# Second chunk's probabilities in fp32 through TensorE, a second engine for the weights' high half, later notices of the other branch

## Chip, cores and metric

One core of one Trainium2 chip. The metric is the device time of one execution in microseconds (us). Engines are named as in the profile: PE is TensorE, DVE VectorE, ACT ScalarE, POOL GpSimd, SP SyncE, whose queue issues the DMAs.

## The reference

Causal sliding-window attention with sink keys (4 sequences, 8 heads, 768 positions, 64 channels a head, window 128, 4 sinks), followed by a two-layer feed-forward part (512 to 2048 to 512, ELU) on all 3072 tokens, in fp32.

```python
scores = scale * np.matmul(q, k.transpose(0, 1, 3, 2))
...
keep = is_sink | in_window
scores = np.where(keep, scores, -1000000000.0)
a = np.exp(scores - np.max(scores, axis=-1, keepdims=True))
a = a / (np.sum(a, axis=-1, keepdims=True) + 1e-09)
attn_out = np.matmul(a, v)
...
h = x @ w_in
g = np.where(h > 0.0, h, alpha * (np.exp(np.minimum(h, 0.0)) - 1.0))
out = g @ w_out
```

## The kernel before

The 3072 tokens are 24 tiles of 128, in nine chunks (`SIZES`): three of two tiles, then six of three. For each chunk `attention(c)` fills the `x` tiles (one for each of the 4 head pairs), and `feed_forward(c, f0, f1, start)` runs the feed-forward part over 16 slices `f` of 128 hidden channels. Chunk 0 and chunk 1 interleave their slices (`PARTS`): slices 0 to 6 of chunk 0, 0 to 12 of chunk 1, then the rest of both.

*Precision.* Products that matter are kept exact to nearly fp32 by splitting each operand into an fp16 high half and an fp16 rest, and adding three of the four partial products. The 32 weight pieces (`weights(k)`, two for each slice) come as fp64 words: ACT makes fp16 upper bits (L307), DVE joins them with the lower bits into an fp32 tile `wv` (L308), ACT copies that into the fp16 high half (L456), and POOL subtracts twice 256 columns for the low half (L457). A load waits until piece k - 5 is done (`AHEAD`).

*Attention of a tile-pair* (a query tile for two heads). A query tile sees its own key tile and the one before (`nb` = 1 in a sequence's first tile, else 2), each with 4 sink columns ahead of it (`KW` = 132); from the third tile of a sequence on (`t >= 2`) the sinks count separately. TensorE makes scores (L601, fp32, in chunks 0 to 3; L595 and L596, fp16, after), DVE adds the mask and takes the minimum (L616), ACT takes the exponential with its sum (L618), ACT or POOL scales the sum (L622), DVE takes the reciprocal (L623). Then there are two ways:

- Chunks with `c < PLAIN` (chunk 0 alone, whose tiles have t = 0 and 1) stay in fp32. POOL multiplies the identity by the reciprocals (`diagonal`, L630), TensorE multiplies the exponentials by that diagonal, which transposes and scales them into an accumulator bank `acc` (L636; banks 0 and 1 in turn, ring `tp`), ACT or DVE brings them to SBUF (L640), and TensorE multiplies them by the loaded fp32 values `vs` (L653).
- All others split. ACT writes the fp16 high half of the scaled probabilities (L668), DVE the rest (L669), POOL the sinks' halves (L675 multiplies, L678 casts, L679 subtracts), all side by side in `pq`; one DMA transpose (L687, issued by SP) turns them into `pt`; TensorE multiplies with the fp16 halves `vh` and `vl` of the values (L701, 12 products for two key blocks) and the sinks (L706, 2 products). `vh` and `vl` are made once for each key tile by ACT (L549) and DVE (L550) from `vs`, which SP loads into a ring of two buffers (L538); `sink_rows` does the same for the sinks of a sequence (L561 to L563).

A head pair's sum in bank `po` becomes the fp16 halves of `x` (ACT L739, DVE L740). In the feed-forward part TensorE makes `h` (L765, 12 products), ACT the exponential (L773), POOL or DVE a step (L775), DVE another (L776), ACT the fp16 high half of `g` (L779), POOL the rest (L786), and TensorE adds to the accumulators `acc` (L793). At a chunk's end the accumulators are stored (L816 to L819).

*What sets the order.* Nothing is ordered by hand. `Plan` collects tasks with an engine, an assumed duration, dependencies and rings of buffers; `order()` lists them through a model of the engines, eight rounds, each with due times worked out backwards from TensorE's order, and keeps the best. On TensorE tasks have positions (`pos`) and four lines (feed-forward, scores, values, transposing), each in its own order. A task may have a second engine (`or_`), and the model takes the one that is free. `slow` over 1 marks DVE tasks that the model delays while POOL works. The assumed durations (`act_us`, `dve_us`, `pool_us`, `PE_T`, `PE_V` and numbers at each task) thus decide the order of every queue. `with_idle_products` puts products of a constant tile (L882) into gaps that the plan shows in the first 100 us.

*The end.* A flag made from range checks decides between this result and a general path. Each engine loads it (L1141) and branches (L1142). `keep_order` gives each engine a notice of the branch's target (`BRANCH_PREFETCH_HINT` in the trace) a number of tasks before its last (`HINTS`).

## Time and profile before

| | us |
|---|---|
| device time, median of 3 runs | 631.98 (630.8 to 632.0) |
| profiled execution's own time | 632.12 |
| its span, first to last instruction | 630.3 |
| PE, DVE, ACT, POOL busy | 608.5, 451.4, 418.8, 291.2 |

The profile is of one execution. Busy time is that of an engine's instructions; idle time is put down to what released it. Matmuls overlap, so that records of one group can be longer than the distance between their starts. The chain of waits gives the time that each piece holds up the end. PEclk is the granted share of TensorE's clock. In instruction rows, "x" gives the number of records.

### The profile page before, as it was taken

The numbers are of one execution on the slowest core, as the hardware profiler recorded it, in microseconds if no ns is written. First come the engines' busy times: TensorE is split into PE (matmuls) and PEld (weight loads), VectorE is DVE, ScalarE is ACT, GpSimd is POOL, SyncE is SP. The second block draws the span as 40 slices with busy tenths as digits, with TensorE's granted clock in tenths as the row PEclk, the third lists the DMA queues.
The fourth block names the chain that finished last, engine by engine and source line by source line (L and its number), as shares of the span: only waits on it lengthen the run. The fifth ranks groups of instructions, "written<-read, shape, count | busy, mean of one in ns | idle before, by whom it ended". The sixth has DMA issues, their size and how long they took to land.

```text
span 630.3 us, 13327 instructions
## 1 busy us (share of the span) xinstructions
PE 608.5 (97%) x4504; PEld 357.1 (57%) x4504; DVE 451.4 (72%) x1187; ACT 418.8 (66%) x1192; POOL 291.2 (46%) x586
## 2 busy tenths in 40 slices
PE   6897999999999999999999999999999999999995
PEld 4564665666666555555555555555555555555552
DVE  7876677868678766688788889788778887542223
ACT  5888887978678866677667767676776676332221
POOL 4885699864345444344334444334334444222221
PEclk9998999999999999999999999999999999999998
DMA  8697967656546765486458865676556854511001
GB/s 288 212 254 189 305 233 208 161 165 176 120 120 137 194 104 103 88 220 174 103 168 189 208 158 148 145 193 144 154 118 134 220 130 100 124 56 30 0 2 54
DMA packets 120863, 95.06 MB, mean 151 GB/s; under 512 B 98132, under 2 KB 98132, under 8 KB 120788
## 3 DMA queue, kind: packets, MB, share of 16 engines
q1 hardware_dynamic: 120788, 94.14, 58.5%
q8 instruction: 37, 0.61, 0.4%
q14 instruction: 38, 0.31, 0.2%
HBM read 63.18 MB, written 7.34 MB: 112 GB/s over the span
## 4 chain that ended last, share of the span: by engine, by line
PE 90%; POOL 4%; DVE 2%; issue 2%; DMA 1%; ACT 0%; POOLq 0%; DVEq 0%; ACTq 0%
PE acc L793 39%; PE h L765 38%; PE po L701 5%; PE s L601 3%; PE s L595 2%; PE s L596 2%; POOL w L457 2%; DMA pt<-pq 1%; PE h L882 1%; DMA vs<-in_vx_dram 1%; POOL pq L630 1%; PE po L706 1%; DVE pt L334 0%; PE acc L636 0%; DVE wv L308 0%
## 5 line engine op out<-in xcount | busy, mean ns | idle before, releaser
L765 PE MATMUL h<-x,w 128*128 128x384 f16 (+1 forms) x1728 | 275.0, 309 | 1.5 <-DVE g L776 1.5
L765 PEld LDWEIGHTS <-w 128*128 128x128 f16 x1728 | 167.8, 98 | 94.9 <-issue 3.4
L786 POOL TENSOR_TENSOR gl<-g,gh 128x384 f16<-128x384 f32 (+1 forms) x144 | 126.0, 876 | 164.1 <-ACT gh L779 142.4
L793 PE MATMUL acc<-w,gh 128*128 128x512 f16 x768 | 192.8, 379 | 1.0 <-POOL w L457 1.0
L773 ACT ACTIVATE g<-h 128x384 f32<-128x384 f32 (+1 forms) x144 | 65.2, 453 | 102.2 <-PE h L765 93.0
L793 PEld LDWEIGHTS <-gh 128*128 128x128 f16 x768 | 72.4, 98 | 70.8 <-ACT g L773 1.4
L793 PE MATMUL acc<-w,gl 128*128 128x512 f16 x384 | 109.2, 379 | 0.0
L669 DVE SCALAR_TENSOR_TENSOR pq<-e,st,pq 128x256 f16<-128x256 f32 (+1 forms) x176 | 95.5, 569 | 15.0 <-ACT pq L668 14.7
L618 ACT ACTIVATE e<-e,st 128x264 f32<-128x264 f32 (+1 forms) x192 | 92.9, 485 | 14.9 <-DVE st L616 14.0
L779 ACT ACTIVATE gh<-g 128x384 f16<-128x384 f32 (+1 forms) x144 | 69.5, 482 | 45.2 <-DVE g L776 43.3
L616 DVE CUSTOM_DVE_ANT_0 e<-s,m 128x264 f32<-128x264 f32 (+1 forms) x192 | 71.8, 405 | 32.8 <-PE s L596 21.5
L776 DVE SCALAR_TENSOR_TENSOR g<-g,h 128x384 f32<-128x384 f32 (+1 forms) x144 | 72.9, 506 | 14.2 <-POOL g L775 12.4
L668 ACT ACTIVATE pq<-e,st 128x256 f16<-128x256 f32 (+1 forms) x176 | 77.5, 482 | 5.1 <-DVE st L623 4.3
L775 POOL TENSOR_SCALAR g<-g 128x384 f32<-128x384 f32 (+1 forms) x79 | 43.2, 547 | 79.1 <-ACT g L773 75.8
L775 DVE TENSOR_SCALAR g<-g 128x384 f32<-128x384 f32 (+1 forms) x65 | 27.1, 417 | 69.0 <-ACT g L773 68.9
L793 PEld LDWEIGHTS <-gl 128*128 128x128 f16 x384 | 37.5, 98 | 46.7 <-POOL gl L786 0.9
L457 POOL TENSOR_TENSOR w<-wv,w 128x256 f16<-128x256 f32 x64 | 48.9, 786 | 6.1 <-ACT w L456 5.5
L524 ACT ACTIVATE kq<-kqs 128x912 f16<-128x912 f32 (+1 forms) x40 | 35.8, 912 | 15.9 <-PE s L596 13.6
L622 POOL TENSOR_SCALAR st<-st 128x2 f32<-128x2 f32 x76 | 19.1, 251 | 49.4 <-ACT e L618 46.0
L701 PE MATMUL po<-pt,vh 128*64 128x128 f16 x656 | 36.1, 222 | 3.4 <-DVE x L740 1.9
L618 ACT ACTIVATION_READ_ACCUMULATOR e<-e,st 128x1 f32 x192 | 36.1, 188 | 0.0
L701 PEld LDWEIGHTS <-vh 128*64 128x64 f16 x656 | 26.6, 109 | 14.6 <-issue 14.0
(92 smaller groups left out, 619.4 us busy)
## 6 DMA issues: line engine op xcount, KB each, us to landing
raw<-in_wt_dram SPq DMA_DIRECT2D x32, 512.0 KB, 4.6
...
```

The source lines that it names most:

```text
L616: red = add("DVE", 0.24 + 0.001 * wd, lambda ee=ee, me=me, sp=sps[e], m=m, wd=wd, to_score=to_score: nc.vector.tensor_tensor_reduce(ee, sp ...
L618: ex = add("ACT", 0.47 + 0.00085 * wd, lambda ee=ee, me=me, rs=rs[:, e : e + 1]: nc.scalar.activation(ee, ee, AF.Exp, bias=me, scale=-1.0, ...
L668: a = add("ACT", act_us(nb * P, True), lambda src=src, hi=hi, re=re: nc.scalar.activation(hi, src, AF.Copy, scale=re), deps=[rr])
L669: b = add("DVE", 0.478 if nb == 2 else 0.33, lambda src=src, hi=hi, lo=lo, re=re: nc.vector.scalar_tensor_tensor(lo, src, re, hi, ALU.mult ...
L701: nc.tensor.matmul(po[e * D : (e + 1) * D, oc], vts[i][x][:, vo : vo + D], pt[:, (2 * e + part) * nb + i, :], start=new, stop=last)
L765: nc.tensor.matmul(hp[:, :n], win[:, part, d, :], xx[:, :n], start=k == 0, stop=k == 3 * ND - 1)
L773: a = add("ACT", act_us(n) + 0.18, lambda gf=gf, hp=hp, sums=sums: nc.scalar.activation(gf, hp[:, :n], AF.Exp, scale=1.0 / G_SCALE, accum_ ...
L775: b = add("DVE", 0.14 + 0.00057 * n, lambda gf=gf: nc.vector.tensor_scalar(gf, gf, -1.0, G_SCALE, ALU.add, ALU.mult), deps=[a], slow=2.1, ...
L776: b = add("DVE", dve_us(n), lambda gf=gf, hp=hp: nc.vector.scalar_tensor_tensor(gf, gf, 0.0, hp[:, :n], ALU.min, ALU.max), deps=[b])
L779: th = add("ACT", act_us(n), lambda gf=gf, gh=gh: nc.scalar.activation(gh[:, :n], gf, AF.Copy), deps=[b])
L786: tls.append(add("POOL", pool_us(cut), lambda gl=gl, gf=gf, gh=gh, cut=cut: nc.gpsimd.tensor_tensor(gl[:, :cut], gf[:, :cut], gh[:, :cut], ...
L793: nc.tensor.matmul(acc[i], gg[:, i * P : (i + 1) * P], wout[:, part, :], start=f == f0 and k == 0, stop=f == f1 - 1 and k == 2)
```

## The change

- `PLAIN` goes from 1 to 2: chunk 1 (tiles with t = 2 and 3) keeps its probabilities in fp32 like chunk 0. Its transposed probabilities go to accumulator bank 2, one buffer (`tp1`).
- Since these tiles have separate sinks, there are new tasks: POOL scales the sinks' exponentials, TensorE transposes them into the free half of bank `po`, ACT or DVE brings them out, and a fifth value product (`sk_raw` by `sink_p`) adds them. The fp32 sink rows (8 partitions) are loaded once for the sequence (`sink_raw`).
- `vs` has four buffers instead of two.
- The copy into the weights' high half may run on ACT or DVE.
- Assumed durations change: `PE_T`, `PE_V`, the weight tasks, the diagonal, the sinks, the making of `x`.
- `HINTS`: 40 tasks instead of 120 before the end on ACT and DVE, 8 instead of 25 on SP.

```diff
 VISIT = 3
 DUP = 4
 AHEAD = 5
-PLAIN = 1
+PLAIN = 2
 IDLE_US, IDLE_FILL, IDLE_UNTIL, IDLE_LEAST = 0.11, 0.6, 100.0, 0.8
 V_AT = 7
 V_AT0 = 5.0
 T_AT = 3.5
-PE_T, PE_V = 0.25, 0.25
-RINGS = dict(tp=2, tp_=2, kqs=2, kq=3, vs=2, vm=2, vt=6, sk=2, e=3, st=6, pq=3, pt=6, g=2, gh=3, x=7, wv=4, s=2, po=1, h=2, wu=2, sv=2, wps=1, raw=6)
+PE_T, PE_V = 0.17, 0.11
+RINGS = dict(tp=2, tp_=2, kqs=2, kq=3, vs=4, sp=2, tp1=1, turned0=1, turned1=1, vm=2, vt=6, sk=2, e=3, st=6, pq=3, pt=6, g=2, gh=3, x=7, wv=4, s=2, po=1, h=2, wu=2, sv=2, wps=1, raw=6)
 
 
 def key_tiles(ch):
...
     vh = rows("vh", [P, VT], F16, RINGS["vt"])
     vl = rows("vl", [P, VT], F16, RINGS["vt"])
     sks = rows("sk", [P, VT], F16)
+    sps_ = rows("sp", [2 * NS, P], F32)
     vm = rows("vm", [P, NP, TOK_MAX], F32)
     es = rows("e", [P, 2, 2 * KW], F32)
     sts = rows("st", [P, 4 + 2 * NS], F32)
...
         ld = add("SP", 0.4, lambda: load_weights(nc, raw, wt[k]), deps=[w_done.get(k - AHEAD, [None])[0]], lat=1.45)
         if wide:
             steps = weight_f32(nc, v, top, raw, 2.0)
-            a = add("ACT", act_us(512), steps[0], deps=[ld])
-            b = add("DVE", 0.13 + 0.00108 * 512, steps[1], deps=[a], slow=1.5)
+            a = add("ACT", 0.77, steps[0], deps=[ld])
+            b = add("DVE", 0.8, steps[1], deps=[a], slow=1.5)
             ring("wu", [a], [b])
             ring("raw", [ld], [a, b])
         else:
             a = b = add("ACT", act_us(512), lambda: nc.scalar.activation(v, raw[:, :512].bitcast(F32), AF.Copy, scale=W_SCALE), deps=[ld])
             ring("raw", [ld], [a])
 
-        th = add("ACT", act_us(512), lambda: nc.scalar.activation(w[k][:, 0, :], v, AF.Copy), deps=[b])
-        tls = [add("POOL", pool_us(256), lambda c=c: nc.gpsimd.tensor_tensor(w[k][:, 1, c], v[:, c], w[k][:, 0, c], ALU.subtract), deps=[th]) for c in (slice(0, 256), slice(256, 512))]
+        th = add("ACT", act_us(512), lambda: nc.scalar.activation(w[k][:, 0, :], v, AF.Copy), deps=[b], slow=2.0, or_=("DVE", 0.13+0.0006*512, lambda: nc.vector.tensor_copy(w[k][:, 0, :], v)))
+        tls = [add("POOL", 0.75, lambda c=c: nc.gpsimd.tensor_tensor(w[k][:, 1, c], v[:, c], w[k][:, 0, c], ALU.subtract), deps=[th]) for c in (slice(0, 256), slice(256, 512))]
         tl = tls[-1]
         ring("wv", [b], tls)
         w_done[k] = th, *tls
...
         x_old.append((lo, hi, users))
 
     later = []
-    raw_of, v_of, sk_of = {}, {}, {}
+    raw_of, v_of, sk_of, raw_sinks = {}, {}, {}, {}
 
     def attention(c):
         ts = CHUNKS[c]
...
                 sk_of[b] = sk, vb, users
             return sk_of[b]
 
+        def sink_raw(b):
+
+            if b not in raw_sinks:
+                st = pool.tile([2 * NS, VT], F32, name=f"sinks{b}")
+                o = SINKS + b * VT
+                raw_sinks[b] = st, add("SP", 0.4, lambda: nc.sync.dma_start(st, vx[0 : 2 * NS, o : o + VT]), lat=0.1)
+            return raw_sinks[b]
+
         k = 0
         for p in range(NP):
             kqp = [split_keys(2 * p + e) for e in range(2 if c >= DUP else 1)]
...
                 rr = add("DVE", 0.17, lambda rs=rs: nc.vector.reciprocal(rs, rs), deps=[rr])
                 if c < PLAIN:
                     dg = pq[:, :4, :].rearrange("p b k -> p (b k)").bitcast(F32).rearrange("p (e k) -> p e k", e=2)
-                    tp = acc[slot("tp")]
+                    tp, tp_ring = (acc[slot("tp")], "tp") if c == 0 else (acc[2], "tp1")
                     ptf = pt.rearrange("p b k -> p (b k)").bitcast(F32)[:, : 2 * nb * P]
+                    far = t >= 2
+                    turned_sinks, sink_p = po[0 : 2 * NS, (nt + j) * P : (nt + j + 1) * P], sps_[slot("sp")][0 : 2 * NS, :] if far else None
 
                     def diagonal(dg=dg, rs=rs):
                         nc.gpsimd.tensor_tensor(dg, ident.unsqueeze(1).to_broadcast([P, 2, P]), rs.unsqueeze(2).to_broadcast([P, 2, P]), ALU.mult)
...
                                 o = (e * nb + i) * P
                                 nc.tensor.matmul(tp[:, o : o + P], e3[:, e, i * KW + NS : (i + 1) * KW], dg[:, e, :], start=True, stop=True)
 
-                    dgs = add("POOL", pool_us(2 * P), diagonal, deps=[rr])
+                    dgs = add("POOL", 0.8, diagonal, deps=[rr])
                     tr = add("PE", PE_T * 2 * nb, turned, deps=[dgs], pos=at[k] + T_AT, line=3)
                     ev = add("ACT", act_us(2 * nb * P), lambda ptf=ptf, tp=tp, n=2 * nb * P: nc.scalar.activation(ptf, tp[:, :n], AF.Copy), deps=[tr, rest_ if pt is pts[-1] else None], or_=("DVE", dve_us(2 * nb * P), lambda ptf=ptf, tp=tp, n=2 * nb * P: nc.vector.tensor_scalar(ptf, tp[:, :n], 1.0, None, ALU.mult)))
-                    ring("e", [r for r, _ in exps], [tr])
-                    ring("st", [r for r, _ in exps], [dgs])
+                    readers, evs = [dgs], [ev]
+                    if far:
+                        sk_raw, sk_ld = sink_raw(g // NT)
+                        sn = add("POOL", 0.25, lambda tmp=tmp, e3=e3, rs=rs: nc.gpsimd.tensor_tensor(tmp, e3[:, :, 0:NS], rs.unsqueeze(2).to_broadcast([P, 2, NS]), ALU.mult), deps=[rr], lock=False)
+                        ts_ = add("PE", 0.2, lambda o=turned_sinks, tmp=tmp: nc.tensor.matmul(o, tmp.rearrange("p e k -> p (e k)"), ident, start=True, stop=True), deps=[sn], pos=at[k] + T_AT + 0.01, line=3)
+                        se = add("ACT", 0.28, lambda o=turned_sinks, sink_p=sink_p: nc.scalar.activation(sink_p, o, AF.Copy), deps=[ts_], or_=("DVE", 0.27, lambda o=turned_sinks, sink_p=sink_p: nc.vector.tensor_scalar(sink_p, o, 1.0, None, ALU.mult)))
+                        readers += [sn, ts_]
+                        evs += [se, sk_ld]
+                        ring("turned" + str(j), [ts_], [se])
+                    ring("e", [r for r, _ in exps], [tr] + readers[1:2])
+                    ring("st", [r for r, _ in exps], readers)
                     ring("pq", [dgs], [tr])
-                    ring("tp", [tr], [ev])
-                    evacs[slot("tp_")] = ev
+                    ring(tp_ring, [tr], [ev])
+                    evacs[slot("tp_") if c == 0 else 2] = ev
                     vts = [vraw(g - nb + 1 + i) for i in range(nb)]
 
-                    def values(po=po, vts=vts, ptf=ptf, j=j, nb=nb, p=p):
+                    def values(po=po, vts=vts, ptf=ptf, j=j, nb=nb, p=p, far=far, sink_p=sink_p, sk_raw=sk_raw if far else None):
                         oc = slice(j * P, (j + 1) * P)
                         for i in range(nb):
                             for e in range(2):
                                 vo = p * P + e * D
-                                nc.tensor.matmul(po[e * D : (e + 1) * D, oc], vts[i][0][:, vo : vo + D], ptf[:, (e * nb + i) * P : (e * nb + i + 1) * P], start=j == 0 and i == 0, stop=j == nt - 1 and i == nb - 1)
-
-                    val = add("PE", PE_V * 2 * nb, values, deps=[ev, *(v[1] for v in vts)], pos=at[k - j + nt - 1] + V_AT0 + 0.01 * j, line=2)
+                                nc.tensor.matmul(po[e * D : (e + 1) * D, oc], vts[i][0][:, vo : vo + D], ptf[:, (e * nb + i) * P : (e * nb + i + 1) * P], start=i == 0, stop=i == nb - 1 and not far)
+                        if far:
+                            nc.tensor.matmul(po[:, oc], sk_raw[:, p * P : (p + 1) * P], sink_p, start=False, stop=True)
+
+                    val = add("PE", PE_V * 2 * nb + (0.2 if far else 0.0), values, deps=[*evs, *(v[1] for v in vts)], pos=at[k - j + nt - 1] + V_AT0 + 0.01 * j, line=2)
                     ring("pt", [ev], [val])
+                    if far:
+                        ring("sp", [se], [val])
                     vals.append(val)
                     for v in vts:
                         v[2].append(val)
...
 
             xh, xl = x_room(qc)
             to_x = X_SCALE / P_SCALE if c < PLAIN else PO_SCALE
-            fa = add("ACT", act_us(qc, True), lambda xh=xh, po=po, to_x=to_x: nc.scalar.activation(xh, po[:, :qc], AF.Copy, scale=to_x), deps=[vals[-1]])
-            fb = add("DVE", dve_us(qc) + 0.1, lambda xh=xh, xl=xl, po=po, to_x=to_x: nc.vector.scalar_tensor_tensor(xl, po[:, :qc], to_x, xh, ALU.mult, ALU.subtract), deps=[fa])
+            fa = add("ACT", act_us(qc)-0.03, lambda xh=xh, po=po, to_x=to_x: nc.scalar.activation(xh, po[:, :qc], AF.Copy, scale=to_x), deps=[vals[-1]])
+            fb = add("DVE", dve_us(qc), lambda xh=xh, xl=xl, po=po, to_x=to_x: nc.vector.scalar_tensor_tensor(xl, po[:, :qc], to_x, xh, ALU.mult, ALU.subtract), deps=[fa])
             ring("po", [vals[0]], [fa, fb])
             users = []
             x_taken(fa, users)
...
 VERBOSE = False
 
 
-HINTS = dict(PE=8, ACT=120, DVE=120, SP=25)
+HINTS = dict(PE=8, ACT=40, DVE=40, SP=8)
 E = mybir.EngineType
 QUEUES = dict(PE=E.PE, ACT=E.Activation, DVE=E.DVE, SP=E.SP)
 
```

## Rows read from the trace of the kernel before

**Rows 1.** Stretches: us, busy (x records) of PE, PEld, DVE, ACT, POOL; PEclk, DMA.

```profile
4.50:32.46 27.96, 24.84 (x176) 16.62 (x176) 22.57 (x90) 21.69 (x63) 18.32 (x33) 1.00 0.77 262
32.46:66.23 33.77, 27.90 (x256) 17.41 (x255) 25.56 (x76) 27.27 (x81) 24.04 (x52) 0.95 0.94 239
66.23:112.00 45.77, 44.72 (x343) 28.83 (x343) 33.25 (x75) 38.88 (x109) 37.99 (x69) 1.00 0.77 239
...
130.00:623.30 493.30, 492.99 (x3592) 282.18 (x3589) 352.86 (x914) 313.75 (x899) 193.03 (x389) 1.00 0.54 131
```

**Rows 2.** Groups of TensorE, 4.5 to 66.3 us; last column: idle before.

```profile
L765 PE MATMUL h<-x,w 128*128 128x256 f16 x84 | 11.5, 293 | 1.5 <-DVE g L776 1.5
...
L636 PE MATMUL acc<-pq,e 128*128 128x128 f32 x48 | 7.6, 296 | 2.1 <-POOL pq L630 2.1
L882 PE MATMUL h<-hot 128*128 128x240 bf16 x29 | 5.4, 343 | 0.0
...
L701 PE MATMUL po<-pt,vh 128*64 128x128 f16 x64 | 4.3, 223 | 3.4 <-DVE x L740 1.9 <-DMA pt<-pq 1.1 <-ACT vh L549 0.4
```

**Rows 3.** Timelines of SP, ACT, PE: start us, us, what [idle before <-releaser].

```profile
38.50 5.11 SPq L687 DMA_TRANSPOSE pt<-pq  x2
43.70 1.01 SPq L538 DMA_DIRECT2D vs<-in_vx_dram  x2
...
47.32 0.63 ACT L549 ACTIVATE vh<-vs 128x512 f16<-128x512 f32 x1 [2.27 <-DMA vs<-in_vx_dram]
...
50.99 0.30 PE L701 MATMUL po<-pt,vh 128*64 128x128 f16 x4 [1.85 <-DVE x L740]
```

**Rows 4.** Chain of waits, pieces of TensorE: start us, us, what, records.

```profile
28.58 1.09 PE acc L636 x8
...
30.68 0.59 PE po L653 x8
...
81.67 0.46 PE po L701 x12
82.12 0.06 PE po L706 x2
82.18 0.34 PE po L701 x12
```

**Rows 5.** Timelines of POOL and DVE.

```profile
17.76 3.01 POOL L457 TENSOR_TENSOR w<-wv,w 128x256 f16<-128x256 f32 x4
...
69.44 0.31 DVE L775 TENSOR_SCALAR g<-g 128x256 f32<-128x256 f32 x1
```

**Rows 6.** Groups of POOL, ACT and DVE, 4.5 to 112 us.

```profile
L630 POOL TENSOR_TENSOR pq<-ident,st 128x256 f32<-128x256 f32 x8 | 6.6, 826 | 3.5 <-DVE st L623 3.1 <-PE acc L636 0.4
...
L679 POOL TENSOR_TENSOR pq<-st,pq 128x8 f16<-128x8 f32 x14 | 3.7, 266 | 1.1
...
L678 POOL CAST pq<-st 128x16 f16<-128x16 f32 x14 | 3.3, 235 | 0.9
...
L668 ACT ACTIVATE pq<-e,st 128x256 f16<-128x256 f32 x28 | 12.5, 494 | 0.2
...
L669 DVE SCALAR_TENSOR_TENSOR pq<-e,st,pq 128x256 f16<-128x256 f32 x26 | 13.1, 540 | 1.5 <-ACT pq L668 1.5
```

**Rows 7.** Lines L1142, L1168 and the last stores, L819: ns, starts; landing, us.

```profile
L1142 SPq EVENT_SEMAPHORE  x8: 17/17/17, 628.4 to 628.9; - x8
...
L1142 SPq COMPARE_BRANCH  x1: 78/78/78, 625.4 to 625.4; - x1
...
L1168 SPq BRANCH_PREFETCH_HINT  x1: 51/51/51, 495.4 to 495.4; - x1
...
L819 SPq DMA_DIRECT2D out_dram<-wv x3: 333/338/338, 622.8 to 624.1; - x3
...
DMA to landing us min/median/max: 2.0/2.7/4.0
```

**Rows 8.** Line L457, 0 to 130 us: shortest/median/longest ns, first and last start.

```profile
L457 POOL TENSOR_TENSOR w<-wv,w x62: 662/672/1202, 13.4 to 126.5; 128x256 f16<-128x256 f32 x62
```

2 lines of the change are left out of this document (1 added, 1 removed).

## Prediction

> **What bounds the kernel now.** I read busy time by stretch first, because a share over the whole span is a mean over stages with different limits. From 130 to 623.3 us TensorE is busy 492.99 of 493.30 us [rows 1]: there the time is a sum of matmuls, and nothing that another engine does can shorten it. The change touches no matmul of that stretch. What it wins or loses lies in the first 112 us and behind the last matmul. From 4.5 to 32.46 us (chunk 0's attention) TensorE is idle 27.96 - 24.84 = 3.1 us, and 29 filler products hide 5.4 more [rows 2]. From 32.46 (the first feed-forward product) to 66.23 (when the first feed-forward of chunk 1 is about to start) it is idle 33.77 - 27.90 = 5.9 us, and from there to 112 it is idle 1.05 us.
>
> What these gaps wait for is the second view [rows 2]. Chunk 1's value products wait 1.9 us for DVE's `x`, 1.1 for a DMA `pt<-pq` and 0.4 for `vh`; chunk 0's feed-forward, held up in the same stretch, 1.5 for `g`. What stands behind that is seen in the queues [rows 3]. SP is in order: from 38.50 it stands 5.11 us at two transposes of chunk 1 and only at 43.70 issues the next loads of `vs`, whose ring has two buffers. ScalarE is in order too: it stands 2.27 us before the fp16 conversion of that `vs` at 47.32, with chunk 1's probabilities and a weight queued behind. At 50.99 TensorE has stood 1.85 us for what comes of them. The granted clock of the stretch averages 0.95 [rows 1]; the levels are 2.4 and 1.2 GHz, so a tenth of 33.77, 3.4 us, ran at the lower one, just after that idle. That cost half of it, 1.7 us.
>
> **The change part by part**, against the profiled execution's 632.1 us (span 630.3 and 1.8 around it; the median of the runs, 631.98, is the same within 0.02%).
>
> *More matmul work, +13.1.* Chunk 1 has 8 tile-pairs (4 head pairs by 2 query tiles, each with two key blocks). Before, one takes 12 + 2 fp16 products: two such in a row are 0.46 + 0.06 and 0.34 + 0.06, or 0.46 each [rows 4]. For after, care is needed with the counts: an fp32 product leaves two records (chunk 0 has 4 x (2 + 4) = 24 transposing products and 48 records [rows 2]). So a tile-pair with two key blocks is the x8 piece and not the x4: transposing 1.09, values 0.59 [rows 4]. Two sink products come on top that no row of before shows. The nearest are 1.09 / 4 = 0.27 (128 stationary columns) and 0.59 / 4 = 0.15 (64, two at a time): bounds 0.30 and 0.54 for both, and I take the middle, 0.42, since one has few stationary columns and the other 128. 1.09 + 0.59 + 0.42 - 0.46 = 1.64, by 8 is +13.1 (12.2 to 14.1). TensorE pays this in full wherever it has no gap to put it in.
>
> *Waits of chunk 1 that go, -7.0.* Eight transposes leave SP's queue, `vs` tiles 1 and 2 need no fp16 halves, tile 3's and the sinks' come later, for chunk 2, and `vs` has four buffers. So ScalarE is no longer held for `vs`, nor SP for DVE's low halves, and weight loads are issued earlier. Of 5.9 us idle and 1.7 of low clock I let 7.0 go, keeping 0.6 for score products that wait for their PSUM ring. Bounds: half, -3.5, and all, -7.6. Next late is then TensorE itself, which has to put the added products between 30 and 66.
>
> *The start, -2.5.* There TensorE has 3.1 us of idle and 5.4 of fillers, 8.5 in all; some 3 of them, with 16 of the 29 fillers, come before 10.4 us, when only the first pairs' scores are there. The rest, 5.5, is the bound of what chunk 1's products and a better order can take; the other is 0. The planner's costs of weight work rise and those of transposing products fall: now four weight halves (3.01 us) stand on POOL from 17.76 [rows 5] before a diagonal that TensorE waits for, 2.1 us in all over chunk 0 [rows 2]. I take a little under half, because ScalarE is busy 21.7 of 28.0 us there [rows 1].
>
> *Relief of ScalarE and DVE, no term.* 16 conversions of 0.49 and 16 subtractions of 0.54 [rows 6] go, 16.5 us; 8 evictions of 512 columns and 8 small ones come, on whichever of the two is free. Neither engine is full in any stretch [rows 1], so this is cover. The sinks' load is one DMA more on SP, beside eight that go.
>
> *POOL, no term.* A tile-pair gains a diagonal (0.83) and loses a cast (0.24) and a subtraction (0.27) [rows 6]: 8 x 0.32 = +2.6 us. In chunk 1's stretch POOL is busy 24.0 of 33.8 [rows 1], room of 9.7 us; without that cover it is rival 1.
>
> *Weights' high half on either engine, -0.5.* Now on ScalarE, it may go to DVE. No row shows that copy there; a DVE operation of half its columns, SBUF to SBUF, took 0.31 [rows 5], so 0.31 to 0.62. It can only move the 1.05 us idle after 66.23 [rows 1]: bounds 0 and -1.05, and I take the middle.
>
> *The notice of the other branch, -0.8.* SP gets it at 495.4, branches at 625.4 and runs its next instruction at 628.4 [rows 7]; the end follows from that. With 8 tasks to go instead of 25 the notice comes later and less can come between. If it works, SP waits for the last store instead, issued at 624.1 and landing 2.7 (median) to 4.0 us later [rows 7], 626.8 to 628.1: -1.6 to -0.3. If not, 0. I take the middle of 0 and -1.6. ScalarE and DVE end before SP, so their notices cost nothing.
>
> Sum: 13.1 - 7.0 - 2.5 - 0.5 - 0.8 = +2.3: 634.4 us. The sum says in one line what decides: TensorE gets 13 us more to do and has some 17 us of gaps and low clock before 112 (8.5 + 7.6 + 1.05), of which 3 can't be filled. To break even it would have to use nearly all.
>
> **The rivals.** *1. POOL becomes the bound (slower still).* Each transposing product now waits for a diagonal on POOL, in order behind weight halves, and chunk 1 has one PSUM bank for it where chunk 0 has two. Chunk 0 pays 2.1 us of waits for 8 diagonals [rows 2]; as much again for chunk 1 and none of the 2.5 won in the start gives 634.4 + 2.1 + 2.5 = 639.0. DVE's copies press the same way: a weight half on POOL takes 0.66 at best, 0.67 at the median and 1.20 at worst [rows 8], so something stretches it at times; 16 of 32 copies on DVE, each stopping POOL for about 0.45, are 7 us, against 7.8 us that POOL is idle from 66 to 112 [rows 1]. It decides where POOL has weight halves queued before chunk 1's diagonals, 30 to 50 us. For it: POOL is busy 38.0 of 45.8 after 66. Against: 9.7 us of room in chunk 1's own stretch. The Trainium skill has the cause as a rule (SBUF — State Buffer, Who interferes with whom): DVE copies of this kind and GpSimd share a port pair, and whichever starts first holds it for its whole instruction. The spread of the halves' durations agrees with it; the planner delays such copies while POOL works, which speaks against the full price.
>
> *2. The gaps are filled nearly whole (faster).* Its place is the start: if chunk 0's diagonals come without weight halves before them and chunk 1's first scores and transposing products follow at once, all 5.5 us there are used, and the other terms reach their bounds too: 632.1 + 13.1 - 7.6 - 5.5 - 1.05 - 1.6 = 629.4. It decides once the first feed-forward product starts 3 us before 32.46 with no gap behind it. For it: no engine but TensorE is over 81% busy in the start [rows 1], and the relief of 16.5 us lies just where ScalarE stood. Against: it needs a plan that holds on the chip to a few tenths of a us, and the plan of before left 17 us.
>
> *3. It just cancels (no change).* The start gives 4.5 instead of 2.5 and all else is as forecast: 632.4; with a tail of -1.2, 632.0. For and against are those of rival 2, asked for less.
>
> That the change doesn't do what it says I leave out: the third accumulator bank is unused by chunks of two tiles.
>
> **How the numbers follow.** Forecast 0.37 (634.4; its own range 633.3 to 637), rival 1 0.11, rival 2 0.32, rival 3 0.20. About 0.2%, 1.3 us, is what a measurement of this kernel can tell from no change (its three runs span 1.2). So faster is rival 2, 0.32; same is rival 3, 0.20; slower is the forecast with rival 1, 0.48. Both signs are likely since +13.1 stands against gaps of 7.6 and 5.5, as large in all if filled whole. The range takes in most of rival 2 (down to 628) and rival 1's milder half (up to 638), which leaves 2 in 10 outside.
>
> **What would show it.** In the profile after: TensorE's records of the transposing line and of the fp32 value line up from 48 to 48 + 8 x 8 = 112 each, 16 on each of two new lines for the sinks, and 112 fp16 value records fewer; no transposes on SP before chunk 2's; no ScalarE wait for `vs` near 47; granted clock 1.00 from 32 to 66; idle there under 1 us; the first feed-forward product at 30 to 32; SP's next instruction less than 1.5 us behind its branch. Wrong would be: fp32 pieces cheaper than 1.09 and 0.59; waits of transposing products over 4 us; idle from 66 on over 3 us; or a stretch from 130 to the end that isn't full or whose matmuls take another sum, since I hold that fixed.

## The result, and the profile after

The changed kernel takes 637.96 us (median of 4 runs, 637.7 to 638.2), the kernel before 631.51 in the same series: a ratio of 1.0103 (95% interval 1.0087 to 1.0119), 6.4 us slower. The profiled execution took 637.9 us (span 636.1), against 632.1 (630.3): +5.8. Forecast was slower, but by 2.3 only.

The lines of the code move by 1 to 24: the key loads L516 are L517 after, the score product L601 is L610, the transposing product L636 is L647, its eviction L640 is L651, the value product L653 is L673, the fillers L882 are L906, DVE's part of `x`, L740, is L764, the feed-forward L765 and L793 are L789 and L817, the fp16 values L701 are L725, the branch L1142 is L1166. New are L656 (sinks transposed) and L675 (sinks' values).

First the stretches of [rows 1], in the same columns:

```profile
4.50:32.46 27.96, 26.49 (x198) 18.35 (x199) 21.85 (x92) 21.54 (x67) 18.73 (x30) 1.00 0.87 302
32.46:66.23 33.77, 33.77 (x265) 23.31 (x265) 19.82 (x56) 21.05 (x66) 20.18 (x37) 1.00 0.38 126
66.23:112.00 45.77, 45.77 (x339) 28.86 (x338) 36.99 (x86) 36.67 (x105) 37.60 (x61) 1.00 0.84 254
...
130.00:629.00 499.00, 497.68 (x3620) 284.86 (x3618) 351.85 (x925) 315.49 (x903) 194.48 (x396) 1.00 0.54 128
```

From 32.46 to 112 us TensorE has no idle time left (5.9 and 1.05 us before), and up to 66 us the granted clock is 1.00 instead of 0.95. The relief came as forecast, and the kernel is slower all the same: what is full now is full of more work. After 130 us 1.3 us are idle, where it was 0.3.

The groups of TensorE from 4.5 to 66.3 us that answer to [rows 2]:

```profile
L647 PE MATMUL acc<-pq,e 128*128 128x128 f32 x112 | 16.5, 288 | 0.6 <-POOL pq L641 0.6
...
L673 PE MATMUL po<-pt,vs 128*64 128x128 f32 x112 | 9.6, 287 | 0.8 <-ACT pt L651 0.6
L789 PE MATMUL h<-x,w 128*128 128x256 f16 x72 | 8.7, 273 | 0.0
L906 PE MATMUL h<-hot 128*128 128x240 bf16 x48 | 7.1, 297 | 0.0
L675 PE MATMUL po<-sp,sinks 8*128 8x128 f32 x16 | 3.9, 321 | 0.0
...
L656 PE MATMUL po<-ident,st 128*8 128x128 f32 x16 | 3.1, 274 | 0.0
```

The record counts are the forecast ones (48 to 112 on both lines, 16 on each new one). The waits of chunk 1 for `x`, `vh` and DMA transposes are gone, and those for POOL fell from 2.1 to 0.6. But there are 48 fillers where there were 29: the start didn't fill.

A tile-pair of chunk 1 in the timeline of TensorE (start us, length, records), with the feed-forward behind it:

```profile
36.74 1.16 PE L647 MATMUL acc<-pq,e 128*128 128x128 f32 x8
37.83 0.39 PE L656 MATMUL po<-ident,st 128*8 128x128 f32 x2
38.14 0.66 PE L673 MATMUL po<-pt,vs 128*64 128x128 f32 x8
38.73 0.48 PE L675 MATMUL po<-sp,sinks 8*128 8x128 f32 x2
39.15 1.48 PE L789 MATMUL h<-x,w 128*128 128x256 f16 x12
```

What a piece takes is the distance to the next start: 1.09 for transposing, 0.31 for the sinks' transposing, 0.59 for the values, 0.42 for the sinks' values. The first and third are those of [rows 4]. The two sink products together take 0.73, where I had 0.42.

Summed over the trace in this way (from each record's start to the next, less the idle time between them, from 4.5 us on), TensorE's time is:

| us | before | after | difference |
|---|---|---|---|
| transposing products | 6.99 | 15.31 | +8.32 |
| fp32 value products | 3.69 | 8.53 | +4.84 |
| sinks: transposing, values | 0 | 2.53 + 3.32 | +5.85 |
| fp16 values and sinks | 28.61 + 7.34 | 25.52 + 6.17 | -4.26 |
| idle 33 to 66 us | 5.87 | 0 | -5.87 |
| feed-forward and scores, same counts | 555.73 | 552.79 | -2.94 |
| before 33 us: idle | 3.12 | 1.47 | -1.65 |
| before 33 us: fillers | 5.20 | 6.65 | +1.45 |
| idle after 66 us | 1.35 | 1.31 | -0.04 |
| rest | 0.51 | 0.51 | 0 |
| last product starts at | 622.92 | 628.61 | +5.69 |

Added work is +14.75; the start gives back 0.2. The idle time of 33 to 66 us gives 5.87, and the products of equal number 2.94. Of these 2.94, 1.7 are the lower clock before, 3.41 us at 0.50 (columns of [rows 1]):

```profile
52.41:55.82 3.41, 3.41 (x16) 2.04 (x15) 0.49 (x2) 2.73 (x10) 1.95 (x7) 0.50 0.94 245
```

The other 1.2 are spread over score and feed-forward products up to 130 us; what made these shorter stays open.

The start has a part that isn't the change's. The same nine fillers behind the same product take 1.91 us to the next start before (10.33) and 1.36 after (9.78):

```profile
8.42 1.98 PE L882 MATMUL h<-hot 128*128 128x240 bf16 x9
...
8.42 1.43 PE L906 MATMUL h<-hot 128*128 128x240 bf16 x9
```

Up to there both starts are alike. Then the pace of equal products doubles, at 9.1 us after and at 11.4 before, where the trace's records of the granted clock begin; the column PEclk leaves out what lies ahead of them. With three key buffers, below, the nine fillers take 1.91 again. So some 1 us of the start's account (0.55 in fillers, about as much in products) is chance of the execution: over all kernels with fillers the doubling comes at 8.7 to 11.6 us.

The tail, lines of the branch, the notice and the last stores, in the columns of [rows 7]:

```profile
L1166 SPq EVENT_SEMAPHORE  x8: 17/17/17, 634.2 to 634.7; - x8
...
L1166 SPq COMPARE_BRANCH  x1: 78/78/78, 631.1 to 631.1; - x1
...
L1192 SPq BRANCH_PREFETCH_HINT  x1: 51/51/51, 552.0 to 552.0; - x1
```

SP's next instruction comes 3.1 us behind its branch, as before (3.0), though the notice now stands 79 us ahead instead of 130. The later notice gave nothing. The last store, on which SP has to wait too, landed 4.0 us after its issue, at 633.7, only 0.4 us before that instruction:

```profile
L843 SPq DMA_DIRECT2D out_dram<-wv x1: 333/333/333, 629.7 to 629.7; - x1
...
DMA to landing us min/median/max: 4.0/4.0/4.0
```

Before, it was the same: issued at 624.1, landed 4.0 us later, 0.3 us before SP went on.

And the waits of TensorE after 66 us, all of them:

```profile
PE s L604 <- DVE kq L527: 1.0, 1, 1.0
PE s L604 <- DVE st L625: 0.3, 1, 0.3
```

The 1.0 us is a new wait, for a key split of a later chunk, which takes the place of the 1.05 that went.

### The profile page after: what moved, and what is told of

The parts are those of the page before. It is cut to its first block, busy times and chain, and to the rows that moved or that the text cites. A ratio compares the mean times of both kernels' runs of the same rounds, so it can differ in the third digit from the quotient of the medians.

```text
span 636.1 us, 13390 instructions
## 1 busy us (share of the span) xinstructions
PE 621.7 (98%) x4571; PEld 367.2 (58%) x4571; DVE 448.5 (71%) x1193; ACT 410.2 (64%) x1178; POOL 287.9 (45%) x566
## 3 DMA queue, kind: packets, MB, share of 16 engines
HBM read 63.20 MB, written 7.34 MB: 111 GB/s over the span
## 4 chain that ended last, share of the span: by engine, by line
PE 95%; DMA 2%; DVE 1%; ACT 1%; issue 0%; POOL 0%; SPq 0%; DVEq 0%; POOLq 0%
PE acc L817 40%; PE h L789 40%; PE po L725 4%; PE s L610 3%; PE s L604 2%; PE s L605 2%; DMA raw<-in_wt_dram 2%; PE acc L647 2%; PE po L673 1%; PE po L675 1%; PE po L730 0%; PE po L656 0%; DVE pt L334 0%; ACT e L627 0%; PE h L906 0%
## 5 line engine op out<-in xcount | busy, mean ns | idle before, releaser
L789 PE MATMUL h<-x,w 128*128 128x384 f16 (+1 forms) x1728 | 273.6, 308 | 0.0
L789 PEld LDWEIGHTS <-w 128*128 128x128 f16 x1728 | 167.4, 98 | 92.5 <-issue 2.7
L817 PE MATMUL acc<-w,gh 128*128 128x512 f16 x768 | 192.4, 380 | 0.0
L817 PEld LDWEIGHTS <-gh 128*128 128x128 f16 x768 | 71.7, 98 | 72.1 <-ACT g L797 3.4
L817 PE MATMUL acc<-w,gl 128*128 128x512 f16 x384 | 109.2, 379 | 0.0
L627 ACT ACTIVATE e<-e,st 128x264 f32<-128x264 f32 (+1 forms) x192 | 93.1, 486 | 15.1 <-DVE st L625 14.1
L693 DVE SCALAR_TENSOR_TENSOR pq<-e,st,pq 128x256 f16<-128x256 f32 x160 | 86.5, 564 | 13.1 <-ACT pq L692 11.9
L692 ACT ACTIVATE pq<-e,st 128x256 f16<-128x256 f32 x160 | 70.8, 481 | 5.4 <-DVE st L632 4.9
L799 POOL TENSOR_SCALAR g<-g 128x384 f32<-128x384 f32 (+1 forms) x73 | 38.8, 531 | 65.0 <-ACT g L797 60.3
L817 PEld LDWEIGHTS <-gl 128*128 128x128 f16 x384 | 37.6, 98 | 45.6 <-POOL gl L810 0.4
L525 ACT ACTIVATE kq<-kqs 128x912 f16<-128x912 f32 (+1 forms) x40 | 36.2, 913 | 16.1 <-PE s L605 13.9
L631 POOL TENSOR_SCALAR st<-st 128x2 f32<-128x2 f32 x70 | 17.7, 254 | 56.0 <-ACT e L627 52.5
L725 PE MATMUL po<-pt,vh 128*64 128x128 f16 x592 | 32.0, 221 | 0.0
L526 DVE SCALAR_TENSOR_TENSOR kq<-kqs,kq 128x528 f16<-128x528 f32 (+1 forms) x40 | 26.6, 666 | 5.4 <-ACT kq L525 4.9
```

Source lines behind the costliest of these rows:

```text
L627: ex = add("ACT", 0.47 + 0.00085 * wd, lambda ee=ee, me=me, rs=rs[:, e : e + 1]: nc.scalar.activation(ee, ee, AF.Exp, bias=me, scale=-1.0, ...
L692: a = add("ACT", act_us(nb * P, True), lambda src=src, hi=hi, re=re: nc.scalar.activation(hi, src, AF.Copy, scale=re), deps=[rr])
L693: b = add("DVE", 0.478 if nb == 2 else 0.33, lambda src=src, hi=hi, lo=lo, re=re: nc.vector.scalar_tensor_tensor(lo, src, re, hi, ALU.mult ...
L725: nc.tensor.matmul(po[e * D : (e + 1) * D, oc], vts[i][x][:, vo : vo + D], pt[:, (2 * e + part) * nb + i, :], start=new, stop=last)
L789: nc.tensor.matmul(hp[:, :n], win[:, part, d, :], xx[:, :n], start=k == 0, stop=k == 3 * ND - 1)
L799: b = add("DVE", 0.14 + 0.00057 * n, lambda gf=gf: nc.vector.tensor_scalar(gf, gf, -1.0, G_SCALE, ALU.add, ALU.mult), deps=[a], slow=2.1, ...
```

## The experiments

Two readings compete. *A*: the added products count in full once chunk 1's waits are gone, so the loss is a sum of products. *B*: something else of the change (durations and order, the copy, the notices, earlier loads) costs the time. Each experiment is an edit of the changed kernel unless it says otherwise; ratios are to the kernel before, run in the same series.

### Which part of the change

**Only the fp32 way undone.** Everything else of the change stays.

```diff
-PLAIN = 2
+PLAIN = 1
```

> The changed kernel with PLAIN back at 1, so that chunk 1 splits its probabilities and turns them by DMA again; the new costs, the four vs buffers, the either-engine copy and the later notices stay. Theory A (the loss is matmul work: 1.9 us more for each of chunk 1's 8 tile-pairs, of which the old gaps took in some 9): the work is gone and the gaps come back, 630 to 633 us. Rival B (the new plan, its costs, the early vs loads or the notices lose the time, and fp32 alone would be even): it stays at 636 to 638.

631.75 us, 1.0006 (0.9991 to 1.0022). The loss goes with the fp32 way. TensorE's useful time (all but idle and fillers) is 600.6 us here and 614.7 in the changed kernel, 14.1 us more. But idle and fillers are 17.5 us here and 9.4 there.

**Only the fp32 way and its rings done.** Durations, copy on ScalarE alone and notices as before.

```diff
-PE_T, PE_V = 0.17, 0.11
+PE_T, PE_V = 0.25, 0.25
...
-HINTS = dict(PE=8, ACT=40, DVE=40, SP=8)
+HINTS = dict(PE=8, ACT=120, DVE=120, SP=25)
```

> The fp32 way for chunk 1 with four vs buffers alone: assumed durations and notices as in the kernel before, the weights' high half on ACT only. Theory A: 636 to 639, the same as the whole change. Rival B: 631 to 633, as the kernel before.

636.74, 1.0092 (1.0075 to 1.0108): the fp32 way alone costs 5.5 us, and the other parts together add 1.2 (0.9 by the ratios). So reading B accounts for a fifth of the loss.

**Old notices.**

```diff
-HINTS = dict(PE=8, ACT=40, DVE=40, SP=8)
+HINTS = dict(PE=8, ACT=120, DVE=120, SP=25)
```

> The changed kernel with the notices of before (120 tasks on ACT and DVE, 25 on SP). The notice does nothing: 637.7 to 638.2, and SP's next instruction still 3 us behind its branch. It does something: 1 us or more to either side.

637.65, 1.011 (1.0093 to 1.0127): no difference. SP's next instruction comes 3.13 us behind the branch. ScalarE's came at 0.47 us here and at 2.70 in the changed kernel; as ScalarE isn't last, the end doesn't see it.

**Nearer notices**, ScalarE's at 2 and SP's at 1.

```diff
-HINTS = dict(PE=8, ACT=40, DVE=40, SP=8)
+HINTS = dict(PE=8, ACT=2, DVE=40, SP=1)
```

> The changed kernel with ScalarE's branch notice at 2 and SyncE's at 1 instead of 40 and 8, so much nearer to the branch. Seen so far: SyncE's first instruction behind the branch comes 2.9 to 3.2 us after it, whether 66 or 23 instructions lie between notice and branch. If the distance was still too long: SyncE's comes at 0.5 us and the time falls by 2 us or more, to 635.0 to 636.0. If distance doesn't matter: 637.5 to 638.2 and 2.9 to 3.2 us again.

637.88, 1.0099 (1.0081 to 1.0117). SP's notice now stands at 629.7 us, 2.2 ahead of the branch, in the lines of the tail:

```profile
L1166 SPq EVENT_SEMAPHORE  x8: 17/17/17, 635.1 to 635.6; - x8
...
L1166 SPq COMPARE_BRANCH  x1: 78/78/78, 631.9 to 631.9; - x1
...
L1192 SPq BRANCH_PREFETCH_HINT  x1: 51/51/51, 629.7 to 629.7; - x1
```

Again 3.2 us. SP's gap stays over three positions of the notice, so my term of -0.8 was no term.

**The copy on ScalarE alone; the old durations.** Two runs, which with two from above make a square.

```diff
-        th = add("ACT", act_us(512), ..., deps=[b], slow=2.0, or_=("DVE", ...))
+        th = add("ACT", act_us(512), ..., deps=[b])
```

> The weights' high half is copied by ScalarE alone again; all else as in the changed kernel. The fp32 way with the old costs, copy and notices took 636.7, so 1.2 us of the loss lie in costs, copy or notices, and the old notices alone gave nothing. If the copy carries the 1.2 us: 636.5 to 637.0. If the assumed durations carry it (they set the order): 637.6 to 638.3. If the copy was a relief: 638.5 or more.

```diff
-PE_T, PE_V = 0.17, 0.11
+PE_T, PE_V = 0.25, 0.25
-            b = add("DVE", 0.8, steps[1], deps=[a], slow=1.5)
+            b = add("DVE", 0.13 + 0.00108 * 512, steps[1], deps=[a], slow=1.5)
...
```

> The changed kernel with the durations that the planner assumed before; the copy on either engine and the new notices stay. Measured so far: everything old but the fp32 way 636.7; the changed kernel 637.8; the changed kernel with the copy on ScalarE alone 639.9. If durations and copy add up, the new durations cost about 3.2 us and the copy on either engine gives 2.1: 634.4 to 635.0. If they don't add up (each gives another order of the work, and what is left is the order's chance): 636.0 to 637.5.

| us | copy on ScalarE alone | on either engine |
|---|---|---|
| old durations | 636.74 | 636.91 |
| new durations | 639.89 | 637.96 |

(The corner 636.74 has the old notices as well, which do nothing.) The copy gives 1.9 us beside the new durations and nothing beside the old; the new durations cost 1.1 or 3.2. So they don't add, as the second guess said; each set leads the planner to another order, and what is in an order that costs this wasn't taken apart. With ScalarE alone 1.5 us of the profiled execution is one wait of a later chunk, in TensorE's waits after 66 us:

```profile
PE po L725 <- DMA pt<-pq: 1.5, 1, 1.5
PE s L604 <- DVE kq L527: 0.9, 1, 0.9
```

### What the added products cost

**Chunk 1's sink tasks left out** (its outputs lack the sinks' part).

```diff
-                        if far:
-                            nc.tensor.matmul(po[:, oc], sk_raw[:, p * P : (p + 1) * P], sink_p, start=False, stop=True)
...
-                    if far:
+                    if False:
                         sk_raw, sk_ld = sink_raw(g // NT)
```

> The changed kernel without chunk 1's sink tasks: the scaling on POOL, the transposing product, its eviction and the fifth value product are left out, so the sinks' share is missing from that chunk's output. They take 0.32 and 0.41 us of TensorE in each of 8 tile-pairs, 5.8 us. Theory A (TensorE has no gap to put them in): 632 to 633 us. Rival B (half of it lies in gaps or fillers): 634.5 to 636.

631.89, 1.0015 (1.0004 to 1.0025): 6.1 us less for 5.85 us of products. They counted in full, as reading A says. (The edit also takes away their tasks on POOL and on ACT or DVE; the next one leaves these in place.)

**Cheap sinks.** The sinks' probabilities go as fp16 halves (as in later chunks) through one fp16 product for the transposing and two for the values.

```diff
-nc.tensor.matmul(o, tmp.rearrange("p e k -> p (e k)"), ident, start=True, stop=True)
+nc.tensor.matmul(o, pq[:, 8, :], ident16, start=True, stop=True)
...
-nc.tensor.matmul(po[:, oc], sk_raw[:, p * P : (p + 1) * P], sink_p, start=False, stop=True)
+for e in range(2):
+    vo = p * P + e * D
+    nc.tensor.matmul(po[e * D : (e + 1) * D, oc], sk[0][:, vo : vo + D], sink_p, start=False, stop=True)
```

> Chunk 1's sink probabilities go in fp16 halves (as those of the later chunks) through one fp16 product for the transposing and two fp16 products for the values, in place of the fp32 ones of 0.32 and 0.41 us a tile-pair. Theory A (every product of chunk 1 counts in full): about 0.15 to 0.2 us a tile-pair in place of 0.73, 8 of them: 4.2 to 4.6 us less, 633.3 to 633.8. Rival P (the preparation on GpSimd, three instructions for one, some 0.65 us a tile-pair more, comes late and TensorE waits for it): 635 to 638, with waits of TensorE for GpSimd of 1.5 us or more in 30 to 66 us.

633.39, 1.003 (1.0019 to 1.004): -4.6, within the range of A. The tile-pair pieces in this kernel's timeline of TensorE (L666 and L687 are the sinks):

```profile
38.16 0.23 PE L666 MATMUL po<-ident,pq 128*128 128x128 f16 x1
38.33 0.66 PE L683 MATMUL po<-pt,vs 128*64 128x128 f32 x8
38.81 0.23 PE L687 MATMUL po<-sp,sk 128*64 128x128 f16 x2
38.97 1.16 PE L649 MATMUL acc<-pq,e 128*128 128x128 f32 x8
```

From start to start the sinks take 0.17 and 0.16 us here. Summed over the trace they take 1.88 us instead of 5.85, so 4.0 of the 4.6 us are these products. TensorE waits 0.6 us for GpSimd up to 66 us, as in the changed kernel, so GpSimd's longer preparation didn't show: rival P falls.

**Transposing by identity.** GpSimd scales the exponentials, and TensorE transposes them by its transposing call, in both chunks.

```diff
-nc.gpsimd.tensor_tensor(dg, ident.unsqueeze(1).to_broadcast([P, 2, P]), rs.unsqueeze(2).to_broadcast([P, 2, P]), ALU.mult)
+nc.gpsimd.tensor_tensor(e3[:, :, 0:wd], e3[:, :, 0:wd], rs.unsqueeze(2).to_broadcast([P, 2, wd]), ALU.mult)
...
-nc.tensor.matmul(tp[:, o : o + P], e3[:, e, i * KW + NS : (i + 1) * KW], dg[:, e, :], start=True, stop=True)
+nc.tensor.transpose(tp[:, o : o + P], e3[:, e, i * KW + NS : (i + 1) * KW], ident)
```

> In chunks 0 and 1 GpSimd multiplies the exponentials themselves by the reciprocal sums and TensorE transposes them against the identity, in place of products with a diagonal made by GpSimd. If a transposition of fp32 costs half of the fp32 product (one record of 0.14 us for two): 8 tile-pairs of chunk 1 at 0.54 us less, 4.3 us less, 633.6; if it costs the same: 637.5 to 638.5 as TensorE's work is unchanged. Rival G: GpSimd's multiplication of 2 x 264 columns takes 1.3 us or more for 0.83, is late in the start and the time grows by 1 us or more above what the transposition gives.

634.82, 1.006 (1.0039 to 1.0081): -3.1. The timeline of TensorE:

```profile
37.78 0.65 PE L647 MATMUL acc<-ident,e 128*128 128x128 f32 x4
38.37 0.39 PE L656 MATMUL po<-ident,st 128*8 128x128 f32 x2
```

Four records instead of eight, and 0.59 us instead of 1.09 to the next start. The Trainium skill (Perfetto Trace Analysis, Transposes) asks for the transposing form in place of a plain product; this trace agrees, with 0.50 us a tile-pair. Of the 4.0 us that chunk 1 saves so, 0.9 is lost again, and so are the 3.4 that chunk 0 saves: idle time and fillers are 14.2 us against 9.4. GpSimd's multiplication took 1.18 us. TensorE's waits up to 66 us name DVE for 1.8 us, which makes `x` (L764), and GpSimd for 0.3, so rival G is not what they show.

**Both together.**

```diff
-                    tr = add("PE", PE_T * 2 * nb, turned, ...)
+                    tr = add("PE", 0.075 * 2 * nb, turned, ...)
...
```

> Transposing by identity on TensorE (GpSimd scales the exponentials) and fp16 halves for chunk 1's sinks together. Theory A (TensorE's work of chunk 1 counts in full): the two gains of 4.5 and 3.0 us add up, 630.1 to 630.8, below the kernel before at 631.5. Rival P (GpSimd's preparation, now 1.1 us and three small instructions a tile-pair in a row, becomes late): 632 to 634, with TensorE waiting for GpSimd over 1.5 us in 30 to 66 us.

632.47, 1.0013 (1.0003 to 1.0022), 2 us short of the sum. Useful time fell by 11.7 us (614.7 to 603.0), but idle and fillers rose by 6.5 (9.4 to 15.9), as the groups of TensorE up to 66.3 us show (L919 are the fillers here, L683 the values, L653 and L667 evictions):

```profile
L919 PE MATMUL h<-hot 128*128 128x240 bf16 x80 | 12.1, 294 | 0.0
...
L683 PE MATMUL po<-pt,vs 128*64 128x128 f32 x112 | 9.5, 286 | 2.6 <-DVE pt L653 1.1 <-ACT pt L653 0.6 <-DVE sp L667 0.6
```

As soon as TensorE has less to do it stands before evictions again. Rival P was right in the time and wrong in the place: the waits are for ACT and DVE, not GpSimd.

**The same with the old durations.**

```diff
-PE_T, PE_V = 0.17, 0.11
+PE_T, PE_V = 0.25, 0.25
...
```

> The same with the durations that the planner assumed before. If the assumed durations cost what the changed kernel shows (1.2 us or more): 629.5 or less. If they only shuffle the order: within 1 us of the run before it.

632.57, 1.0015 (1.0001 to 1.0028): no difference. In the profiled execution (633.75) the first feed-forward product comes at 37.6 us (33.0 in the run before it), and the time of the kernel is the same: when that product comes says little, since work that is done ahead of it isn't lost.

### What holds the start

**Later loads of V.** In the changed kernel SP issues the loads of key tiles 2 and 3 of V early, ahead of keys and weights.

```diff
-ld = add("SP", 0.4, lambda: nc.sync.dma_start(st, vx[:, g * VT : (g + 1) * VT]), lat=dma_us(P * VT * 4))
+ld = add("SP", 0.4, lambda: nc.sync.dma_start(st, vx[:, g * VT : (g + 1) * VT]), deps=[w_done[2][0]] if g in (2, 3) else [], lat=dma_us(P * VT * 4))
```

> In the changed kernel SyncE issues the loads of key tiles 2 and 3 of V at 5.2 us, ahead of weights and keys that the first feed-forward product needs; here these two loads wait for the third weight block. Theory S (the start is held by its transfers, and the early V loads push the weights back): the first feed-forward product comes 1 to 2.5 us earlier than 33.4 and the time falls by 0.5 to 1.5 us, to 636.4 to 637.4. Rival W (TensorE's added work of chunk 1, 1.4 us of which stands ahead of that product, is the delay; the loads have room): the first product moves by less than 0.5 us and the time stays within 0.4 us of 637.9.

637.8, 1.0104 (1.0085 to 1.0123): nothing, and the first feed-forward product comes at 33.0 instead of 33.4. Theory S falls.

**No fillers.**

```diff
-IDLE_US, IDLE_FILL, IDLE_UNTIL, IDLE_LEAST = 0.11, 0.6, 100.0, 0.8
+IDLE_US, IDLE_FILL, IDLE_UNTIL, IDLE_LEAST = 0.11, 0.6, 0.0, 0.8
```

> The changed kernel without filler products (6.7 us of them stand before 33 us). If the fillers only stand where TensorE would be idle: 637.3 to 638.3 and as many us of idle more; if they hold up real products by standing before them: 635.5 to 637.2; if TensorE's clock falls without them: 639 or more, with a granted clock under 1.00 in the first 66 us.

640.08, 1.013 (1.0107 to 1.0154): 2.1 us slower. The stretches of its trace (columns of [rows 1]):

```profile
4.50:20.00 15.50, 12.04 (x58) 8.64 (x59) 10.51 (x49) 9.30 (x30) 5.67 (x10) 0.96 0.82 307
20.00:26.00 6.00, 5.78 (x28) 4.00 (x28) 3.65 (x16) 4.26 (x16) 4.67 (x9) 0.50 0.79 247
26.00:33.00 7.00, 6.63 (x43) 4.23 (x40) 4.95 (x20) 4.39 (x16) 4.29 (x7) 0.79 0.57 180
```

After the first 15 us, of which TensorE was idle 3.5, the granted clock is 0.50, its lower level, from 20 to 26 us. But this is the longest of four executions (642.36). Another took 639.92 with a mean granted clock of 0.998, that of the changed kernel, so this stretch isn't what the median lost. What the same trace shows earlier bears on it: a score product of four records takes 1.18 us to the next start,

```profile
11.20 1.25 PE L610 MATMUL s<-kqs 64*128 64x264 f32 x4
12.38 0.69 PE L673 MATMUL po<-pt,vs 128*64 128x128 f32 x4
```

and in the changed kernel, behind 16 fillers, 0.64:

```profile
10.97 0.71 PE L610 MATMUL s<-kqs 64*128 64x264 f32 x4
11.61 0.44 PE L673 MATMUL po<-pt,vs 128*64 128x128 f32 x4
```

Without fillers the pace doubles at 15.3 us instead of 9.1. So with the fillers TensorE is at its higher pace earlier, and they aren't what the start loses; that this alone makes the 2.1 us is likely and not shown.

**Three key buffers.** SP stands for score products before it may reload one of the two key buffers, with weight loads behind it in its queue.

```diff
-kqs=2
+kqs=3
```

> Key buffers of chunks 0 and 1 three instead of two. In the changed kernel SyncE stood 9.1 us, six times, from 4.5 to 34 us for score products before it could issue a key load, with weight loads in order behind it; TensorE's idle and fillers before 33 us make 8.1 us. Theory K (the start is held by this ring): SyncE's waits for score products nearly go, idle and fillers before 33 us fall to 5 or 6, and the time by 1.5 to 3 us, to 635.0 to 636.3. Rival E (the start is held by the chain of a tile-pair through DVE, ScalarE and GpSimd, with weights among it): idle and fillers stay at 7.5 to 9, and the time within 0.7 us of 637.8.

635.66 (634.2 to 638.5), 1.006 (1.0037 to 1.0084): 2.3 us less. The first 28.5 us, in the columns of [rows 1], of the changed kernel:

```profile
4.50:33.00 28.50, 27.03 (x202) 18.82 (x202) 22.39 (x93) 21.89 (x68) 19.27 (x32) 1.00 0.87 303
```

and with three buffers:

```profile
4.50:33.00 28.50, 28.14 (x212) 20.00 (x213) 19.43 (x90) 18.95 (x67) 13.19 (x26) 1.00 0.65 226
```

Idle and fillers before 33 us fall from 8.1 to 6.1 us. SP's waits in its queue before key loads (L517) for score products (L610), in us in total, times and longest, of the changed kernel up to 34 us:

```profile
SPq L517 <- PE s L610: 9.1, 6, 3.1
```

and with three buffers:

```profile
SPq L517 <- PE s L610: 17.5, 6, 4.7
```

Theory K is right in the time and in the unused time, and wrong in the waits: they got longer, not shorter. A wait of SP for a key that is needed later costs nothing, and with a third buffer the key that is needed next is there already. The load of chunk 1's first keys and the first score product that reads them, in the changed kernel:

```profile
18.99 0.33 SPq L517 DMA_DIRECT2D kqs<-in_kq_dram  x1
24.44 0.72 PE L610 MATMUL s<-kqs 64*128 64x264 f32 x4
```

and with three buffers:

```profile
12.71 0.33 SPq L517 DMA_DIRECT2D kqs<-in_kq_dram  x1
23.05 0.72 PE L610 MATMUL s<-kqs 64*128 64x264 f32 x4
```

With two buffers this load is issued behind chunk 0's next to last pair, lands 5.3 us later, at 24.3, and the product follows 0.1 us after. With three it is issued 6.3 us earlier and holds nothing. So the sum of the waits couldn't say what the ring costs. Two of the 2.5 us that I had given to the start are to be had, but by this edit and not by the change. The profiled execution was the longest of its five (638.5), as long as the changed kernel: after 66 us it has 18 fillers (2.0 us), a wait of 1.8 us for a transpose by DMA and a granted clock of 0.97. So how the 2.0 us of the start become the median's 2.3 is not shown.

**Cheaper products with three key buffers.** Two runs: cheap sinks, and transposes with cheap sinks.

> Cheap sinks (633.4) with three key buffers. Theory K: 630.4 to 632.0. Rival E: 632.7 to 634.1.

632.16, 1.0007 (0.9996 to 1.0019): -1.2, between the two and nearer to K.

> Transposing by identity, cheap sinks (632.5) and three key buffers. TensorE's useful work is 603.0 there against 614.7 in the changed kernel, but its idle and fillers rose from 9.4 to 15.9 us. Theory K: they fall by 2 to 4 and the time to 628.5 to 630.5, below the kernel before. Rival E: 631.8 to 633.2.

631.79, 1.0007 (0.9995 to 1.002): -0.7, within the noise, at the lower end of E. With useful time of 603.8 and idle and fillers of 13.9 us it only draws level with the kernel before (602.9 and 15.5).

**The kernel before with three key buffers; cheap sinks, three buffers and old durations.** Same edits as above.

> The kernel before with three key buffers. The third buffer took 2.2 us from the changed kernel and 1.2 from the one with cheap sinks. If the ring of two holds the start whatever chunk 1 does: 629.5 to 630.7, faster than both kernels. If it helps only where chunk 1's products can move into the start (before, chunk 1 waits for transposes on SyncE's queue): 631.2 to 632.5.

631.61, 1.0001 (0.9989 to 1.0013): nothing. The third buffer helps with the fp32 way and not without it, as it would if it let chunk 1's products move up.

> Cheap sinks and three key buffers with the durations that the planner assumed before. The old durations gave 0.9 us in the changed kernel. If that is a property of them: 631.0 to 631.6. If it was the chance of one order: anything from 631.5 to 633.5.

632.12, 1.0011 (1.0001 to 1.002): as with the new durations (632.16), though one duration, that of the sinks on POOL, stayed new. Over two pairs of kernels the durations gave nothing, so what they gave in the changed kernel looks like the chance of one order.

No kernel of these beat the one before. The useful time (before and in the last line, it contains 1.7 us of a stretch at the lower clock) of TensorE and what it leaves unused (idle and fillers, from 4.5 us on) in the profiled executions:

| kernel | time, us | useful | unused |
|---|---|---|---|
| before | 631.5 | 602.9 | 15.5 |
| fp32 way undone | 631.75 | 600.6 | 17.5 |
| changed | 637.96 | 614.7 | 9.4 |
| no sink tasks | 631.89 | 607.4 | 10.1 |
| cheap sinks | 633.39 | 609.3 | 10.4 |
| transposes | 634.82 | 606.9 | 14.2 |
| both | 632.47 | 603.0 | 15.9 |
| cheap sinks, three buffers | 632.16 | 609.0 | 8.8 |
| both, three buffers | 631.79 | 603.8 | 13.9 |

## Why the prediction was wrong in its size

The direction and the bound (TensorE) held, and so did the mechanism but for the start and the notice. The sum was 3.5 us short. The step that failed most is the room at the start, 2.3 us of it; the sum of the products, by the price of the sinks (1.65), the notice (0.9) and the copy (0.5) failed too, and 1.8 that the waits gave beyond their term covered part of it. By its terms:

- *More matmul work, +13.1: it was +14.75, beyond the bound of 14.1.* Transposing (1.04 a tile-pair on average), values (0.60) and the removed fp16 products (0.53, where I had 0.46) were right within 0.07. The sinks were not: 0.73 for 0.42, that is 2.5 us over 8 tile-pairs. I bounded them by products of 128 and 64 columns in long pieces and took few columns for a discount. The product with 8 stationary columns took 0.31 to 0.32, and the one over 8 rows 0.41 to 0.42, both above the 0.27 that I held for the dearer end.
- *Waits of chunk 1, -7.0: -8.8.* All 5.87 us of idle went and the 1.7 of the low clock, -7.6, just the bound. The step was right and a little cautious. The other 1.2, in products whose number stays the same, I had in no term; that they came is luck.
- *The start, -2.5: -0.2.* Idle fell by 1.65 us, but 1.45 more went into fillers. I counted fillers as room that chunk 1's products could take, without asking whether their keys would be there: a ring of two key buffers lets SP load the next pair's keys only when a score product has read an earlier pair's. The later loads of V and the fillers were not the cause; the third buffer gave 2.0 of the unused 8.1 us and 2.3 us of the median time.
- *The copy, -0.5: 0 in all.* The 1.05 us after 66 went, and 1.0 came back as a wait for a key split after 130. In the square above the copy is worth 1.9 us beside the new durations, and what these lead to costs as much or more: the two weren't separable into terms.
- *The notice, -0.8: +0.1.* SP's gap behind the branch stays at 3 us. My bound was wrong too: I took the -1.6 from the median landing of the three last stores, 2.7 us, but the last one itself took 4.0, so by my own reckoning no more than 0.3 was to be had.

The price of a short piece stood in the trace of before, in rows that I didn't price from:

```profile
27.23 0.71 PE L636 MATMUL acc<-pq,e 128*128 128x128 f32 x4
27.87 0.71 PE L601 MATMUL s<-kqs 64*128 64x264 f32 x4
```

Four transposing records take 0.64 us to the next start, eight 1.09 [rows 4]. That is 0.11 a record and some 0.2 for the piece, and for a piece of two records an estimate of 0.4. The two sink pieces would have come to 0.8; they took 0.73.

With the measured terms: 14.75 - 8.8 - 0.2 + 0 + 0.1 = +5.85, against +5.8 in the span. The measured time lies just inside the 638 of my wider range, which I had drawn for rival 1; its cause is not rival 1.

Of the rivals, 1 is excluded: TensorE waits 0.6 us for POOL up to 66 us. Nor did DVE's copies stop POOL: 14 of 32 went to DVE, and POOL's 64 weight halves took 0.66, 0.67 and 1.21 us (shortest, median, longest), 0.66, 0.67 and 1.20 before. Rival 2 was right for the waits of chunk 1 and wrong for its own place, the start. The condition that I had written for it, a first feed-forward product 3 us before 32.46, was no good sign: it came at 33.4 after the change and at 30.7 with the old durations, copy and notices, and the run with 37.6 was as fast as the one with 33.0.

What stays open: which of the engines in a tile-pair's chain holds the 6 us that the start still leaves unused with three key buffers (some 3.4 of it are the 16 fillers before 10.4 us), and why SP's notice doesn't help. That the notice's target isn't what SP fetches was not tried, nor whether SP stands for its last store: in every trace that store lands 3.9 to 4.05 us after its issue and 0.1 to 0.6 before SP goes on.
